# A persistent tile of weighted sums, two column groups visited per weight for two batches together, and another order of the head

## The chip, the cores and the metric

The kernel runs on one core of one Trainium2 chip. A core has a matrix engine (TensorE, PE in the profile, with its weight loads as PEld), a vector engine (DVE), a scalar engine (ACT), a general engine (POOL) and SyncE (SP), which only issues transfers. Each engine works through its own list of instructions in order and waits on semaphores for the others. The metric is the time of one execution on the device in microseconds (us), as a median of runs; the profile is of one execution of its own.

## The reference

A cross attention between a sequence and a small state, then a gated layer over all rows:

```python
def _attn_ref(x, state):                      # x (8, 8, 512, 64), state (8, 8, 32, 64)
    scores = scale * np.matmul(x, state.transpose(0, 1, 3, 2))
    scores = scores - scores.max(-1, keepdims=True)
    a = np.exp(scores)
    a /= a.sum(-1, keepdims=True) + 1e-09
    xread = np.matmul(a, state)
    ...                                       # the same the other way round: sread from x
    return np.concatenate([xread, sread], axis=2)

def _moe_ref(x, w_gate, w_val, w_out):        # x (4352, 512), d_ff 1536
    gate = 1.0 / (1.0 + np.exp(-(x @ w_gate)))
    val = x @ w_val
    return gate * val @ w_out
```

The rows of a batch are its 512 sequence positions and its 32 state positions, with the 8 heads side by side as 512 columns.

## The kernel before

**Reassociation.** The rows that go into the gated layer are softmax weights times state. The kernel doesn't form them for the sequence positions: for each batch it first multiplies the state with the gate and value weights (the tile `SW`, "weighted sums", 1536 columns for each of two sides `e` and each weight `w`), and then the softmax weights `aT` with `SW`. A block `f` of 128 hidden columns is then four matmuls of 128x512: two for the gate (`gvp`, first half) and two for the value.

**A visit** (`sw_visit`, through `sw_pair` or `sw_mm`) makes weighted sums of one batch: 8 matmuls, each on 64 rows and 32 columns of the array with 512 moving columns, into two PSUM banks; two copies (`sw_cp`, on ACT or DVE) bring them to `SW`. With `sw_pair` the 512 columns are 256 of the gate and the same 256 of the value weights, so a visit needs both weights. `sw_wide` makes three visits for 768 columns, for batch 2 in the head.

**A block** is `gv_mm` (or `gv_half` for one of its two halves), then `gv_th` (tanh on ACT), then `gv_glu` (DVE). The output product runs as seven products of sums and differences of quarter matrices: `h_sum` and `s_sum` build sums of the glu tile, `ht_sum` differences of the output weights, `h_mm` and `w_mm` the products, `w_add` and `w_keep` put them together.

**Softmax.** For batch 0 by quarters: `Sq_mm`, `Sq_exp`, `nq_sum`, `nq_mul`; for others by halves: `S_mm`, `S_exp`, `n_sum`, `n_mul`; `at_Eb` casts the exponentials on POOL (4 casts). `aT_mm` and `aT_cp` transpose the softmax weights on PE for batches 0 and 1; `aT_dma` does so by transfers on SP for later ones. `rd_mm` and `rd_fin` are the read of the state side.

**Loads.** All weights are loaded by POOL and cast on the way: `load_w(w, lo, n)` for n columns of the gate (0) or value (1) weights from column lo, `load_wo` for a third of the output weights, `load_sb` for two batches' states (transposed later by `sT_mm`). The columns come in the groups 256 (256 to 511), 1024, 0 and 1280 of 256 columns each, and 512 (512 to 1023).

**Order.** The schedule is manual: each engine runs its instructions in the order in which the list of calls in the kernel has them. The *head* is the long list from line 563 to line 837; it covers batches 0 and 1 and prepares batch 2. From there `step(b, f)` repeats for the batches 2 to 7 and the rows of all states. PSUM has eight banks, named G0, G1, OU, S0 to S3 and AT, and each call names its bank, so a call also waits for the one that last read its bank. In the profile L293 and L286 are visits, L343 the blocks of `gv_mm`, L355 those of `gv_half`, L442 the products of the head, L234 `aT_mm`, L543 `sT_mm`, L104 `load_w`, L527 `load_sb`, L107 `load_wo`, L200 `at_Eb`, L193 `nq_mul`, L227 `n_mul`, L111 the zeroing of a tile.

Of the kernel before, what the change touches and what calls it, by code (L numbers as in the profile page):

```python
# [8 lines left out]
FP = mybir.dt.float32  # L9
# [7 lines left out]
def kernel(  # L17
# [116 lines left out]
    def xT_cp(b, j, cp, n=1):  # L134
        cp(xT_tile(b)[:, j:j + n], held["xT", b, j])
# [161 lines left out]
    def sw_visit(b, lo, n, p0, p1, *ws):  # L297

        if b not in SWs:
            SWs[b] = fp.tile((128, 2, 2, dff), BF, name="SW", bufs=2)  # L300
        pss = [p[0].tile((128, 512), FP, name="swp", tag=p[1]) for p in (p0, p1)]
        if not ws:
            sw_pair(pss, b, lo, n)
            for e in range(2):
                sw_left[b, lo, 2, e] = (SWs[b][:, e, :, lo:lo + n], pss[e].rearrange("p (w n) -> p w n", w=2))
        for w in ws:
            sw_mm(pss, b, w, lo, n, 0)
            for e in range(2):
                sw_left[b, lo, w, e] = (SWs[b][:, e, w, lo:lo + n], pss[e][:, :n])

    def sw_wide(b, v, *places):

        if b not in SWs:
            SWs[b] = fp.tile((128, 2, 2, dff), BF, name="SW", bufs=2)
# [345 lines left out]
    gv_glu(0, 2)  # L660
    gv_mm(0, 9, AT, S3)
    gv_mm(1, 3, G1, S0)
    gv_th(0, 9)
    sw_cp(1, 1024, 2, 1, vec)
    gv_mm(1, 2, AT, G0)
    gv_glu(0, 9)
    gv_th(1, 3)
    gv_glu(1, 3)
    nc.scalar.activation(pre[:, 0:1], ones, AF.Exp)
    gv_th(1, 2)  # L670
    sT_mm(2, S1)
    gv_mm(1, 8, S2, S3)
    zero(sTz, pool)
    gv_th(1, 8)
    gv_glu(1, 2)
    load_x(2, nc.gpsimd)
    gv_mm(0, 8, S0, G0)
    sw_visit(0, 0, 256, AT, S2)
    sT_cp(2, vec)
    gv_glu(1, 8)  # L680
    sw_cp(0, 0, 2, 0, vec)
    gv_th(0, 8)
    sw_cp(0, 0, 2, 1, act)
    sw_visit(0, 1280, 256, S1, G1)
    sw_cp(0, 1280, 2, 1, act)
    sw_cp(0, 1280, 2, 0, vec)
    load_wo(0)
    gv_mm(1, 9, OU, S0)
    gv_th(1, 9)
    gv_glu(1, 9)  # L690
    gv_mm(0, 1, S2, S3)
    sT_mm(3, G1)
    sT_mm(1, AT)
    gv_th(0, 1)
    gv_glu(0, 1)
    sT_cp(3, act)
# [24 lines left out]
    gv_mm(0, 5, G1, OU)
    rd_fin(1)
    gv_th(0, 5)
    gv_mm(0, 7, S1, S3)
    sw_cp(1, 512, 1, 0, vec)
    sw_cp(1, 512, 1, 1, act)
    gv_glu(0, 5)
    nc.gpsimd.memset(xs[:, :, :, D:], 1.0)
    gv_mm(0, 4, S0, G0)
    gv_th(0, 7)  # L730
    gv_glu(0, 7)
    gv_th(0, 4)
    gv_glu(0, 4)
    gv_mm(0, 6, S1, G1)
    cast_x(2, pool, 4, 4)
    load_wo(2)
    gv_th(0, 6)
    sw_wide(2, 1, S3, OU, S0, G0, S2, AT)
    gv_glu(0, 6)
    sw_cp(2, 1, 0, 1, act)  # L740
    sw_cp(2, 1, 0, 0, vec)
    sw_cp(2, 1, 1, 1, vec)
    sw_cp(2, 1, 1, 0, act)
    gv_mm(1, 5, S1, G1)
    gv_th(1, 5)
    gv_glu(1, 5)
    sw_cp(2, 1, 2, 0, act)
    h_sum(0, 1, vec)
    gv_mm(1, 6, OU, S3)
    sw_visit(1, 1280, 256, S1, G0)  # L750
    gv_th(1, 6)
    sw_cp(2, 1, 2, 1, act)
    sw_visit(1, 0, 256, S2, S0)
    sw_cp(1, 1280, 2, 0, act)
    h_sum(2, 0, pool)
    h_sum(2, 1, vec)
    sw_cp(1, 1280, 2, 1, act)
    gv_mm(1, 4, G1, OU)
    gv_glu(1, 6)
# [17 lines left out]
    h_mm(5, 0, G1)
    S_mm(2, 0, OU)
    h_mm(5, 1)
    ht_sum(2, vec)  # L780
    h_sum(1, 0, vec)
    load_x(3, nc.sync)
    ht_sum(1, vec)
    gv_th(1, 10)
    h_mm(7, 0, S0)
    gv_glu(1, 10)
    sw_cp(1, 0, 2, 0, act)
    h_sum(3, 0, pool)
    w_keep('V1', 1)
    h_mm(6, 0)  # L790
    S_exp(2, 0)
    n_sum(2, 0)
    n_mul(2, 0, pool)
    S_mm(2, 1, G0)
    aT_dma(2, 0)
    S_exp(2, 1)
    gv_mm(1, 0, OU, S2)
    h_sum(3, 1, vec)
    gv_th(1, 0)
    h_mm(6, 1)  # L800
    w_keep('U2', 1)
    n_sum(2, 1)
    ht_sum(3, vec)
    n_mul(2, 1, pool)
    aT_dma(2, 1)
    h_U4()
    gv_mm(1, 1, G0, S1)
    h_mm(2, 0, S3)
    gv_glu(1, 0)
    h_mm(2, 1)  # L810
    gv_th(1, 1)
    cast_x(3, pool, 4, 4)
    h_mm(3, 0)
    gv_glu(1, 1)
    cast_x(3, pool, 0, 4)
    at_xT_dma(3)
    h_mm(7, 1)
    w_add(2, 'V1', w_res(0, 0)[:, :, lo_])
    h_mm(3, 1)
    sw_wide(2, 0, AT, S2, S1, G0, S3, OU)  # L820
    w_add(7, 'U4', w_res(0, 1)[:, :, hi_])
    sw_cp(2, 0, 1, 1, act)
    sw_cp(2, 0, 0, 1, act)
    sw_cp(2, 0, 2, 0, act)
# [10 lines left out]
    at_Eb(2)  # L835
    rd_mm(2, S2)
    rd_fin(2)

    order = {0: "1a", 1: "1b", 2: "2a", 3: "2b", 4: "6a", 5: "6b", 6: "5a", 7: "5b", 8: "7a7b", 9: "3a", 10: "3b4a", 11: "4b"}
    last_order = {0: "1a", 1: "1b", 2: "2a", 3: "2b", 4: "6a", 5: "6b", 6: "5a", 7: "5b", 8: "7a", 9: "7b", 10: "3a", 11: "3b"}  # L840

    def sw_six(b, v):

        if b not in SWs:
            SWs[b] = fp.tile((128, 2, 2, dff), BF, name="SW", bufs=2)
# [190 lines left out]
```

## Time and profile before

| | us |
|---|---|
| median of 3 runs (212.85 to 213.03) | 212.94 |
| the profiled execution | 213.18 |
| its span, first to last instruction | 211.4 |
| PE busy in the span (96%) | 203.4 |
| DVE busy (76%) | 160.5 |
| ACT busy (61%) | 129.8 |
| POOL busy (37%) | 78.6 |

The granted clock of TensorE is 1.00 throughout. A row of the timeline reads: start and duration in us, engine (a q behind it marks an engine's issue of a transfer that doesn't count as busy), line, operation, written tile <- read tiles, shape, number of instructions merged, and in brackets the idle time of the engine before it and what ended that. A row of the DMA issues has the size of one and the time from issue to landing. Matmuls overlap, so a row of many lasts longer than the distance to the next row.

### The profile page before, as it was taken

To read this page: it belongs to the slowest core of one execution; us is meant where nothing else is said; L and a number is where in the kernel's file an instruction comes from. 1 tells how busy PE (TensorE), PEld (TensorE's weight loads), DVE (VectorE), ACT (ScalarE), POOL (GpSimd) and SP (SyncE) were. 2 spreads that over 40 slices of the span, in tenths; PEclk is the share of its full clock that TensorE was granted. 3 is DMA by queue.
4 is the path that set the end of the run, shared out by engine and by line. 5 is a ranking of instruction groups with operands and counts; after the bars stand their busy time and mean duration, and the time that the engine had idled before them with its cause. 6 is when DMAs were issued, how large, how long until landed. Compare 5 with 4: busy or idle time off the path is not lost.

```text
span 211.4 us, 5331 instructions
## 1 busy us (share of the span) xinstructions
PE 203.4 (96%) x2089; PEld 132.1 (62%) x2089; DVE 160.5 (76%) x308; ACT 129.8 (61%) x244; POOL 78.6 (37%) x104
## 2 busy tenths in 40 slices
PE   7679999999999999999999999999999999999993
PEld 2445443677666656565656565656566666788982
DVE  2788889998987788578876887687848876864682
ACT  4978888754767477855786578647774673233210
POOL 8899358599042705900391029301500000000010
PEclk9999999999999999999999999999999999999999
DMA  6999999671689942995923611274110500130044
GB/s 205 180 192 191 227 277 179 113 214 38 80 220 349 123 93 85 301 104 141 312 65 48 195 78 28 58 110 164 29 31 0 202 2 0 74 128 0 3 172 125
DMA packets 40921, 27.14 MB, mean 128 GB/s; under 512 B 23617, under 2 KB 38721, under 8 KB 40897
## 3 DMA queue, kind: packets, MB, share of 16 engines
q1 hardware_dynamic: 30544, 19.47, 37.1%
q0 software_dynamic: 9920, 7.01, 20.4%
q10 hardware_dynamic: 432, 0.33, 0.6%
q8 instruction: 16, 0.26, 0.6%
q14 instruction: 9, 0.07, 0.2%
HBM read 18.35 MB, written 8.91 MB: 129 GB/s over the span
## 4 chain that ended last, share of the span: by engine, by line
PE 91%; DMA 4%; POOL 2%; issue 1%; DVE 0%; POOLq 0%
PE gvp L355 30%; PE outp L425 29%; PE gvp L343 10%; PE gvp L358 5%; PE outp L442 4%; DMA wgv<-in_moe_w_val_dram 4%; PE swp L286 4%; PE outp L484 2%; PE swp L293 2%; PE Sp L147 1%; PE outp L467 1%; POOL wgv L104 1%; PE rdp L262 1%; POOL xf L100 1%; PE rdp L265 0%
## 5 line engine op out<-in xcount | busy, mean ns | idle before, releaser
L369 DVE SCALAR_TENSOR_TENSOR glu<-th,gvp 128x512 bf16<-128x512 f32 (+1 forms) x108 | 70.1, 655 | 36.6 <-PE gvp L355 13.7
L364 ACT ACTIVATE th<-gvp 128x512 f32<-128x512 f32 (+1 forms) x108 | 62.1, 578 | 49.5 <-PE gvp L355 34.8
L355 PE MATMUL gvp<-aT,SW 128*128 128x512 bf16 x288 | 77.4, 379 | 0.1
L329 ACT CAST SW<-swp 128x512 bf16<-128x512 f32 x83 | 46.7, 593 | 9.3 <-PE swp L286 8.3
L425 PEld LDWEIGHTS <-Sm 128*128 128x128 bf16 x324 | 31.7, 98 | 12.6
L355 PEld LDWEIGHTS <-SW 128*128 128x128 bf16 x288 | 26.7, 98 | 17.3 <-issue 3.1
L200 POOL CAST Eb<-E 128x256 bf16<-128x256 f32 x32 | 12.8, 438 | 52.0 <-ACT E L167 52.0
L425 PE MATMUL outp<-tw,Sm 128*128 128x256 bf16 x240 | 31.8, 273 | 0.0
L425 PEld LDWEIGHTS <-glu 128*128 128x128 bf16 x240 | 23.5, 98 | 10.2
L425 PE MATMUL outp<-wo,glu 128*128 128x256 bf16 x168 | 22.9, 273 | 0.0
L343 PE MATMUL gvp<-aT,SW 128*128 128x512 bf16 x96 | 22.6, 379 | 0.0
L509 POOL DMA_DIRECT2D out_dram<-res x1 | 0.6, 613 | 50.3 <-DVE res L433 50.3
L227 POOL TENSOR_TENSOR ab<-E,ri 128x512 bf16<-128x512 f32 x13 | 14.3, 1100 | 11.8 <-DVE ri L210 7.1
L407 DVE TENSOR_TENSOR Sm<-glu 128x768 bf16<-128x768 bf16 (+1 forms) x34 | 18.0, 536 | 0.0
L433 DVE SCALAR_TENSOR_TENSOR res<-outp,U 128x512 f32<-128x512 f32 x22 | 15.1, 686 | 1.2 <-PE outp L442 0.9
L343 PEld LDWEIGHTS <-SW 128*128 128x128 bf16 x96 | 8.7, 98 | 10.5 <-issue 1.6
L116 POOL CAST xb<-xf 128x1024 bf16<-128x1024 f32 x12 | 13.2, 1126 | 2.3 <-DMA xf<-in_x_dram 2.3
L358 PE MATMUL gvp<-xb,wgv 128*128 128x256 bf16 x96 | 12.6, 273 | 0.0
L167 ACT ACTIVATE E<-Sp 128x512 f32<-128x512 f32 x14 | 8.4, 599 | 6.9 <-PE Sp L147 5.7
L425 PE MATMUL outp<-wo,Sm 128*128 128x256 bf16 x84 | 11.5, 273 | 0.0
L358 PEld LDWEIGHTS <-wgv 128*128 128x128 bf16 x96 | 9.3, 98 | 1.3
L251 POOL CAST xs<-xf 128x1024 bf16<-128x1024 f32 x10 | 10.1, 1039 | 0.0
(106 smaller groups left out, 221.6 us busy)
## 6 DMA issues: line engine op xcount, KB each, us to landing
out_dram<-res SPq DMA_DIRECT2D x14, 512.0 KB, 3.3
xf<-in_x_dram SPq DMA_DIRECT2D x5, 1024.0 KB, 7.5
wo<-in_moe_w_out_dram POOLq DMA_DIRECT2D x3, 512.0 KB, 8.1
xf<-in_x_dram SPq DMA_DIRECT2D x4, 256.0 KB, 3.7
wgv<-in_moe_w_gate_dram POOLq DMA_DIRECT2D x4, 256.0 KB, 7.3
wgv<-in_moe_w_val_dram POOLq DMA_DIRECT2D x4, 256.0 KB, 8.7
xf<-in_x_dram POOLq DMA_DIRECT2D x1, 1024.0 KB, 10.1
xf<-in_x_dram POOLq DMA_DIRECT2D x2, 256.0 KB, 5.9
```

The source lines that it names most:

```text
L116: cp(xbs[b].rearrange("p c h d -> p h c d")[:, lo:lo + n], (xhs if b in xhs else xfs)[b][:, lo:lo + n])
L200: nc.gpsimd.tensor_copy(Ebs[b][:, c], E1s[b][:, c])
L227: (nc.gpsimd if eng is pool else nc.vector).tensor_tensor(half(b, i, abs_), e1, ri.unsqueeze(len(ri.shape)).to_broadcast(e1.shape), ALU.mult)
L329: cp(*sw_left.pop((b, lo, w, e)))
L343: nc.tensor.matmul(ps, SWs[b][:, g, w, fs], aTs[b][:, :, g], start=(g == 0), stop=(g == 1))
L355: nc.tensor.matmul(ps, SWs[b][:, g, w, fs], aTs[b][:, :, g], start=(g == 0), stop=(g == 1))
L358: nc.tensor.matmul(ps, (wg, wv)[w][:, j, fs], held["XS"][:, j], start=(j == 0), stop=(j == 3))
L364: nc.scalar.activation(th, held["gv", b, f][0], AF.Tanh, scale=0.5)
L369: nc.vector.scalar_tensor_tensor(glus[b][:, f], held["th", b, f], 1.0, held["gv", b, f][1], ALU.add, ALU.mult)
L407: eng.tensor_tensor(S_(b, t)[:, i], a, c, op)
L425: nc.tensor.matmul(wps[key][:, c], lhs[:, i, c * 128:(c + 1) * 128], rhs[:, i], start=(first and c == 0 and i == 0), stop=(i == NF // 2 - ...
L433: nc.vector.scalar_tensor_tensor(to, wps[key], 0.5, held["w", name], ALU.mult, ALU.add)
```

## The change

- The tile `SWp`, which lives through the whole kernel, holds the weighted sums of two batches; batch b uses half b % 2. Before, `SW` was a tile of a pool with two buffers.
- `sw_joint(w, lo, ...)` visits 256 columns of one weight for the batches 0 and 1 together: 16 matmuls with 256 moving columns into two banks, and two copies into both halves of `SWp`. Four of these (gate and value, groups 256 and 1024) stand in place of four visits of the two batches.
- Blocks 3 and 2 of batch 0 are issued by halves (`gv_half`).
- The rest of the head has another order and other banks, and some operations change engines.

```diff
+    SWp = wp.tile((128, 2, 2, 2, dff), BF, name="SWp")
...
         if b not in SWs:
-            SWs[b] = fp.tile((128, 2, 2, dff), BF, name="SW", bufs=2)
+            SWs[b] = SWp[:, b % 2]
...
+    def sw_joint(w, lo, p0, p1):
+
+        pss = [p[0].tile((128, 2, 256), FP, name="swp", tag=p[1]) for p in (p0, p1)]
+        for b in range(2):
+            SWs[b] = SWp[:, b]
+            for j in range(4):
+                for e in range(2):
+                    rows = slice(e * 64, (e + 1) * 64)
+                    nc.tensor.matmul(pss[e][j * Ns:(j + 1) * Ns, b], sTd[rows, b, 2 * j + e, e],
+                                     (wg, wv)[w][rows, j, lo:lo + 256], start=True, stop=True)
+        for e in range(2):
+            sw_left["j", lo, w, e] = (SWp[:, :, e, w, lo:lo + 256], pss[e])
```

The head as it is after the change, up to the read of batch 1 (lines with a plus are new at their place; the lines that they replace are left out here), and of what follows the lines that change engines or banks:

```diff
     Sq_mm(0, 2, S1)
+    Sq_mm(0, 0, G1)
+    warm(3, S0)
+    xT_cp(0, 1, vec)
+    Sq_mm(0, 1, S3)
+    xT_mm(0, 3, AT)
+    load_w(0, 256, 256)
+    Sq_exp(0, 0)
+    xT_mm(1, 0, OU, 2)
+    Sq_exp(0, 1)
+    xT_cp(0, 3, vec)
     Sq_exp(0, 2)
     load_w(1, 256, 256)
+    Sq_mm(0, 3, S3)
+    xT_cp(1, 0, vec, 2)
     load_w(0, 1024, 256)
+    load_w(1, 1024, 256)
+    S_mm(1, 0, S0)
     nq_sum(0, 2)
+    Sq_exp(0, 3)
+    nq_sum(0, 3)
+    S_exp(1, 0)
+    xT_mm(1, 2, G0, 2)
+    at_Eb(0)
+    rd_mm(0, G1)
+    nq_mul(0, 2, pool)
+    sw_joint(0, 256, OU, S2)
     nq_sum(0, 0)
     nq_sum(0, 1)
+    nq_mul(0, 3, vec)
+    n_sum(1, 0)
+    nq_mul(0, 0, pool)
+    xT_cp(1, 2, act, 2)
+    nq_mul(0, 1, pool)
+    sw_cp("j", 256, 0, 1, act)
+    S_mm(1, 1, S0)
+    sw_joint(1, 256, S3, G0)
+    load_sb(2)
+    aT_mm(0, AT)
+    rd_fin(0)
+    S_exp(1, 1)
+    sw_cp("j", 256, 0, 0, act)
+    aT_cp(0, 1, act)
+    sw_cp("j", 256, 1, 1, act)
+    sw_cp("j", 256, 1, 0, act)
+    aT_cp(0, 0, vec)
     load_w(1, 0, 256)
+    sw_joint(0, 1024, S0, G1)
+    gv_half(0, 3, 0, AT)
+    n_sum(1, 1)
+    gv_th(0, 3)
+    n_mul(1, 1, vec)
+    sw_cp("j", 1024, 0, 0, act)
     load_w(1, 1280, 256)
+    gv_half(0, 2, 0, S2)
+    sw_joint(1, 1024, G0, S1)
+    n_mul(1, 0, pool)
+    sw_cp("j", 1024, 1, 0, act)
+    gv_half(0, 3, 1, S3)
+    sw_cp("j", 1024, 0, 1, vec)
+    sT_mm(2, AT)
     load_w(0, 1280, 256)
+    aT_mm(1, OU)
+    gv_th(0, 2)
     load_w(0, 0, 256)
+    sw_cp("j", 1024, 1, 1, vec)
+    sT_cp(2, vec)
+    gv_mm(0, 8, G1, G0)
+    aT_cp(1, None, vec)
+    nc.scalar.activation(pre[:, 0:1], ones, AF.Exp)
     load_sb(1)
+    gv_mm(0, 9, S1, S2)
+    gv_glu(0, 3)
+    gv_th(0, 8)
+    gv_th(0, 9)
+    gv_mm(1, 3, S0, S3)
+    gv_half(0, 2, 1, G1)
+    gv_mm(1, 8, OU, AT)
+    gv_glu(0, 8)
+    at_Eb(1)
+    gv_glu(0, 9)
     load_sb(3)
+    gv_th(1, 3)
+    gv_glu(0, 2)
+    gv_th(1, 8)
+    gv_mm(1, 2, S1, G0)
     load_w(0, 512, 512)
+    sw_visit(0, 1280, 256, S2, S0)
+    gv_th(1, 2)
+    gv_glu(1, 3)
+    zero(sTz, pool)
+    sw_visit(0, 0, 256, OU, S3)
+    gv_mm(1, 9, G1, S1)
+    sw_cp(0, 0, 2, 0, act)
+    gv_glu(1, 8)
+    sT_mm(3, AT)
+    sw_cp(0, 0, 2, 1, vec)
     load_w(1, 512, 512)
+    sT_mm(1, OU)
+    gv_th(1, 9)
     sw_cp(0, 1280, 2, 1, act)
     sw_cp(0, 1280, 2, 0, vec)
+    sT_cp(1, act)
+    gv_mm(0, 0, S3, S2)
+    gv_mm(0, 1, G1, S0)
+    load_x(2, nc.gpsimd)
+    gv_glu(1, 2)
+    gv_th(0, 0)
+    sw_visit(0, 512, 512, S3, OU, 0)
+    gv_glu(1, 9)
+    sT_cp(3, vec)
+    gv_th(0, 1)
+    sw_visit(1, 512, 512, G0, S1, 0)
+    gv_mm(0, 10, G1, AT)
+    sw_cp(0, 512, 0, 0, act)
+    gv_glu(0, 0)
+    sw_cp(0, 512, 0, 1, vec)
+    gv_mm(0, 11, S3, S2)
     load_wo(0)
+    sw_cp(1, 512, 0, 1, act)
+    sw_cp(1, 512, 0, 0, act)
     gv_glu(0, 1)
+    sw_visit(0, 512, 512, S1, OU, 1)
+    gv_th(0, 11)
     gv_th(0, 10)
+    sw_visit(1, 512, 512, S0, G0, 1)
+    sw_cp(0, 512, 1, 1, vec)
+    sw_cp(0, 512, 1, 0, act)
+    nc.gpsimd.memset(xs[:, :, :, D:], 1.0)
+    rd_mm(1, S3)
+    rd_fin(1)
...
+    h_sum(2, 1, pool)
...
+    ht_sum(2, pool)
...
+    n_mul(2, 0, pool)
...
+    h_sum(3, 1, pool)
...
+    h_mm(7, 0, S0)
...
+    gv_glu(1, 1)
+    sw_wide(2, 0, OU, S3, G0, S2, S1, AT)
...
+    n_mul(2, 1, vec)
...
-    h_sum(2, 1, vec)
...
-    ht_sum(2, vec)
...
-    h_sum(3, 1, vec)
...
-    n_mul(2, 1, pool)
...
-    sw_wide(2, 0, AT, S2, S1, G0, S3, OU)
...
```

More of the change, by code (lines that the diff above doesn't have):

```diff
@@ L313, in sw_wide @@
         if b not in SWs:
-            SWs[b] = fp.tile((128, 2, 2, dff), BF, name="SW", bufs=2)
+            SWs[b] = SWp[:, b % 2]
         lo = 768 * v
@@ L670 @@
[L670 to L684, printed above, removed]
+    sw_visit(0, 1280, 256, S2, S0)
[5 more added lines that the diff above has]
+    sw_cp(0, 0, 2, 0, act)
@@ L731 @@
+    load_wo(1)
+    gv_mm(0, 7, G1, OU)
+    gv_th(0, 7)
+    pad(2, 6)
+    gv_glu(0, 11)
+    gv_mm(0, 4, G0, S1)
     gv_glu(0, 7)
     gv_th(0, 4)
-    gv_glu(0, 4)
[L734 to L738, printed above, removed]
-    gv_glu(0, 6)
-    sw_cp(2, 1, 0, 1, act)
[L741 to L747, printed above, removed]
+    load_wo(2)
@@ new lines @@
+    gv_mm(0, 5, S3, S0)
+    cast_x(2, pool, 0, 4)
+    gv_mm(0, 6, S2, AT)
+    gv_th(0, 5)
+    gv_th(0, 6)
+    cast_x(2, pool, 4, 4)
+    gv_glu(0, 4)
+    gv_glu(0, 5)
+    at_xT_dma(2)
+    sw_wide(2, 1, S1, OU, G1, G0, S0, S2)
+    gv_glu(0, 6)
+    gv_mm(1, 5, S3, AT)
+    sw_cp(2, 1, 0, 0, vec)
+    sw_cp(2, 1, 1, 1, act)
+    gv_mm(1, 7, G0, S1)
+    gv_th(1, 5)
+    gv_th(1, 7)
+    sw_cp(2, 1, 2, 0, vec)
+    sw_cp(2, 1, 2, 1, vec)
+    gv_mm(1, 4, S3, G0)
+    sw_cp(2, 1, 1, 0, act)
@@ L748 @@
+    gv_glu(1, 5)
+    gv_glu(1, 7)
+    sw_visit(1, 1280, 256, S2, G1)
+    gv_th(1, 4)
+    sw_visit(1, 0, 256, AT, S0)
+    gv_mm(1, 6, S3, S1)
+    sw_cp(1, 1280, 2, 1, vec)
+    sw_cp(2, 1, 0, 1, act)
+    gv_glu(1, 4)
+    S_mm(2, 0, OU)
+    h_sum(2, 1, pool)
+    sw_cp(1, 1280, 2, 0, act)
     h_sum(0, 1, vec)
-    gv_mm(1, 6, OU, S3)
-    sw_visit(1, 1280, 256, S1, G0)
+    load_x(3, nc.sync)
+    gv_mm(1, 11, G1, G0)
     gv_th(1, 6)
-    sw_cp(2, 1, 2, 1, act)
-    sw_visit(1, 0, 256, S2, S0)
@@ L777 @@
[L777 to L799 removed]
+    h_sum(0, 0, pool)
+    h_mm(2, 0, S2)
@@ new lines @@
+    ht_sum(0, vec)
+    gv_th(1, 11)
+    h_sum(1, 0, pool)
+    h_mm(1, 0, S3)
+    h_mm(1, 1)
+    sw_cp(1, 0, 2, 1, act)
+    S_exp(2, 0)
+    h_sum(1, 1, vec)
+    w_keep('V1', 1)
+    h_sum(3, 0, pool)
+    S_mm(2, 1, OU)
+    ht_sum(2, pool)
+    h_mm(2, 1)
+    h_mm(5, 0, G1)
+    ht_sum(1, vec)
+    n_sum(2, 0)
+    gv_glu(1, 11)
+    w_add(2, 'V1', w_res(0, 0)[:, :, lo_])
+    h_sum(2, 0, vec)
+    sw_cp(1, 0, 2, 0, act)
+    h_mm(5, 1)
+    n_mul(2, 0, pool)
+    S_exp(2, 1)
+    h_sum(3, 1, pool)
@@ L800 @@
+    n_sum(2, 1)
+    h_mm(6, 0)
+    gv_glu(1, 6)
     h_mm(6, 1)
     w_keep('U2', 1)
-    n_sum(2, 1)
+    cast_x(3, pool, 0, 4)
+    gv_mm(1, 0, S2, OU)
+    h_U4()
+    gv_th(1, 0)
+    gv_mm(1, 10, S0, G0)
+    gv_th(1, 10)
+    gv_mm(1, 1, S1, AT)
+    h_mm(7, 0, S0)
+    aT_dma(2, 0)
+    gv_th(1, 1)
+    gv_glu(1, 0)
+    gv_glu(1, 10)
+    gv_glu(1, 1)
+    sw_wide(2, 0, OU, S3, G0, S2, S1, AT)
+    h_mm(7, 1)
+    h_mm(3, 0)
+    n_mul(2, 1, vec)
     ht_sum(3, vec)
-    n_mul(2, 1, pool)
@@ L844, in sw_six @@
         if b not in SWs:
-            SWs[b] = fp.tile((128, 2, 2, dff), BF, name="SW", bufs=2)
+            SWs[b] = SWp[:, b % 2]
         lo = 768 * v
```

143 lines of the change are left out of this document (5 added, 138 removed).

## The prediction

> **What bounds the kernel now.** I read the page first, then stretches of the span, then TensorE (PE) in order of time, then POOL and the DMA issues. The profiled execution took 213.18 us around this span, 0.24 us over the median of 212.94:
>
> ```profile
> span 211.4 us, 5331 instructions
> ```
>
> Busy time by stretch (PE, PEld, DVE, ACT, POOL, then granted clock, DMA share, GB/s):
>
> ```profile
> 16.00:28.00 12.00, 12.00 (x115) 5.46 (x100) 10.18 (x17) 9.92 (x21) 8.36 (x12) 1.00 1.37 231
> 28.00:54.00 26.00, 25.98 (x343) 15.59 (x343) 23.97 (x43) 17.93 (x35) 19.26 (x20) 1.00 0.73 149
> ...
> 34.00:35.00 1.00, 1.00 (x6) 0.41 (x6) 1.00 (x3) 1.00 (x3) 1.00 (x2) 1.00 0.73 87
> 35.00:36.00 1.00, 1.00 (x20) 0.33 (x18) 1.00 (x3) 1.00 (x3) 0.96 (x1) 1.00 1.19 184
> 36.00:37.00 1.00, 1.00 (x20) 0.36 (x5) 1.00 (x3) 1.00 (x4) 0.52 (x1) 1.00 1.25 206
> ```
>
> From 16 us to the end of the head (54 us) PE has no idle time: any stall that the new order adds there is paid in full, and there is nothing to win there by waiting less. What can be won lies before 16 us. PE in order of time, and the one weight load (PEld) that waited for a transfer:
>
> ```profile
> 15.62 0.63 PE L293 MATMUL swp<-wgv,tw 64*32 64x512 bf16 x16 [0.27 <-DMA wgv<-in_moe_w_val_dram]
> 16.18 0.62 PE L234 MATMUL aTp<-ident,ab 128*128 128x128 bf16 x8
> 16.64 3.62 PE L343 MATMUL gvp<-aT,SW 128*128 128x512 bf16 x16
> 20.09 0.40 PE L543 MATMUL stp<-ident,tw 128*128 128x64 bf16 x8
> 20.32 1.89 PE L343 MATMUL gvp<-aT,SW 128*128 128x512 bf16 x8
> 22.14 0.62 PE L293 MATMUL swp<-wgv,tw 64*32 64x512 bf16 x16
> ...
> 28.03 1.05 PE L286 MATMUL swp<-wgv,tw 64*32 64x512 bf16 x24
> ```
>
> ```profile
> 28.46 0.14 PEld L286 LDWEIGHTS <-tw 64*32 64x32 bf16 x16 [0.31 <-DMA wgv<-in_moe_w_val_dram]
> ```
>
> So the dense stretch starts at 15.62, when the value columns 1024 land, and at 28.46 PE meets a transfer again: value columns 512 to 1023, the largest load. At that point the kernel is just in time. Everything after 28.46 is the same work in both kernels.
>
> **What POOL issues, and when.** POOL issues all weight loads, in the order of the list:
>
> ```profile
> 7.28 0.74 POOL L527 DMA_DIRECT2D tw<-in_state_dram  x1
> 8.01 0.77 POOL L104 DMA_DIRECT2D wgv<-in_moe_w_val_dram  x1
> 9.35 1.19 POOL L193 TENSOR_TENSOR ab<-E,riq 128x256 bf16<-128x256 f32 x2 [0.57 <-DVE riq L188]
> 10.48 0.81 POOL L104 DMA_DIRECT2D wgv<-in_moe_w_val_dram  x1
> 11.28 1.42 POOL L200 CAST Eb<-E 128x256 bf16<-128x256 f32 x4
> 12.65 0.74 POOL L104 DMA_DIRECT2D wgv<-in_moe_w_gate_dram  x1
> 13.41 1.06 POOL L227 TENSOR_TENSOR ab<-E,ri 128x512 bf16<-128x512 f32 x1
> 14.40 0.80 POOL L104 DMA_DIRECT2D wgv<-in_moe_w_gate_dram  x1
> 15.21 1.47 POOL L527 DMA_DIRECT2D tw<-in_state_dram  x2
> 16.67 0.77 POOL L104 DMA_DIRECT2D wgv<-in_moe_w_gate_dram  x1
> 17.40 0.79 POOL L104 DMA_DIRECT2D wgv<-in_moe_w_val_dram  x1
> 18.13 1.47 POOL L200 CAST Eb<-E 128x256 bf16<-128x256 f32 x4
> 19.50 1.84 POOL L111 MEMSET sTz<- 128x2048 bf16 x1
> ```
>
> **The change, part by part.**
>
> *Joint visits.* Four visits of 8 matmuls of 512 columns become four of 16 matmuls of 256: the columns that stream stay the same (two old visits, x16, take 0.56 us: 15.62 to 16.18). Eight copies of 128x512 stay eight copies of 128x512. What changes is that a visit needs one weight alone. The four first weight loads keep their places on POOL, so the value columns 1024 still land at about 15.5 and release the last joint visit at about 15.62. By then the new order has done the gate visit of 1024 as well (0.2 to 0.3 us gained) and four matmuls of the hidden layer (the gate halves of blocks 3 and 2), as many as before (both halves of block 3).
>
> *PE from 15.62.* Joint visit with its change of tile shape 0.56, one half block 0.43 (16 matmuls from 16.64 to 20.09 give 0.216 each, so 0.43 for a half and 0.86 for a block), the state transpose 0.23, the transposes of the softmax weights 0.46, five and a half blocks 4.75: 22.05, against 22.14 before with the same seven blocks done. The head start is eaten by the change of shape for one more visit. Taken as nothing; bounds -0.3 and +0.3 (ACT, which makes most of the copies here, would be late by half a copy). From there: two visits 0.56, a block 0.86, two state transposes 0.47, two blocks 1.73, so the gate visits of the columns 512 are wanted at 25.8; with their 0.56 and two blocks 1.73, the value visits at 28.2. Before, they ran at 28.46. Mode changes are as many as before; the warm matmuls stay three.
>
> *POOL, the step that decides.* Behind the fourth weight load the list now has the four casts of Eb, three multiplications instead of two, and only then the load of the second state group. The casts wait for the last quarter exponential. Before, two of these ended at 9.53:
>
> ```profile
> 8.66 0.87 ACT L182 ACTIVATE E<-Sp 128x256 f32<-128x256 f32 x2
> ```
>
> The new order has the same four at about the same place, so 9.6. Then: casts 1.42, multiplications 3 x 0.595 = 1.79: 12.8. State load 0.74, two value loads 0.77 + 0.81: 15.1. The batch 1 multiplication 1.06: 16.2. Two gate loads 0.74 + 0.80, a state load 0.74: 18.5. Casts of batch 1 1.47: 19.95. State load 0.74, gate 512 load 0.77: issued at 20.7, over at 21.5. The zeroing of sTz 1.84: the value 512 load is issued at 23.3 instead of 17.40. Behind it stand the input of batch 2 and the three output weight loads, which come later by 2 to 3 us at most and are queued in the DMA stream anyway.
>
> How long does such a load take when the stream isn't full? Issue to landing of the loads of 512 KB (gate 512, value 512, the last of the output weights):
>
> ```profile
> wgv<-in_moe_w_gate_dram POOLq DMA_DIRECT2D x1, 512.0 KB, 8.1
> ```
>
> ```profile
> wgv<-in_moe_w_val_dram POOLq DMA_DIRECT2D x1, 512.0 KB, 11.0
> ```
>
> ```profile
> wo<-in_moe_w_out_dram POOLq DMA_DIRECT2D x1, 512.0 KB, 6.4
> ```
>
> ```profile
> 32.34 0.74 POOL L107 DMA_DIRECT2D wo<-in_moe_w_out_dram  x1
> ```
>
> The first two were queued behind others. The third is the nearest: issued at 32.34, with the stream running dry before it (87 GB/s in 34 to 35, 206 in 36 to 37), it took 6.4 us. So value 512 lands between 23.3 + 6.4 = 29.7 and, if I take off 1.2 us for tails and an earlier POOL, 28.5; gate 512 at 26 to 27.1 instead of wanted 25.8, a stall which the second wait swallows. I take 29.4, so the value visits start at 29.45: +1.0 us against 28.46. Bounds 0 (backlog hides the late issue) and +1.6.
>
> The Trainium skill, "DMA: Bandwidth & Descriptors", section "Anatomy of one DMA — SWDGE (gpsimd) path", gives about 2.0 us and the bytes at 436 GB/s for one such load. For 1 MB read, that is an estimate of 4.4 us by that page, hence 27.7 and no wait at all; the 6.4 us measured here speak against it, and I go by the row.
>
> *The head behind 28.46.* The same blocks, products and visits, at the same PE cost. What moves: one sum of the glu tiles (768 columns) and one difference of the output weights (1536 columns) from DVE to POOL, one multiplication from POOL to DVE.
>
> ```profile
> 42.35 2.29 POOL L407 TENSOR_TENSOR Sm<-glu,Sm 128x768 bf16<-128x768 bf16 x1 [2.39 <-DVE Sm L407]
> ```
>
> ```profile
> 39.98 1.82 DVE L400 TENSOR_TENSOR tw<-wo 128x1536 bf16<-128x1536 bf16 x2
> ```
>
> ```profile
> L369 DVE SCALAR_TENSOR_TENSOR glu<-th,gvp 128x512 bf16<-128x512 f32 (+1 forms) x108 | 70.1, 655 | 36.6 <-PE gvp L355 13.7
> ```
>
> On DVE the difference cost 0.91; on POOL, at twice the 2.29 of half its width, up to 4.6, with about 2 us to spare before product 7 needs it. DVE is at 23.97 of 26 us in this stretch, and the second wide visit now ends on bank AT, which waits for the last glu operation (0.66) of batch 1: 0.2 us, bounds 0 and 0.6. The second transposes of batch 2's softmax weights go out on SP behind a multiplication that now sits late on DVE; before, the block that needs them started here:
>
> ```profile
> 53.57 0.61 PE L355 MATMUL gvp<-aT,SW 128*128 128x512 bf16 x2
> ```
>
> That start moves with PE; taken as nothing, bounded by 0 and 0.3.
>
> *The persistent tile SWp* replaces two rotating buffers of the same size: nothing, since each batch still has its half.
>
> **Sum.** 213.18 + 1.0 + 0.2 = 214.4 for the profiled execution; 0.24 less for the median: 214.1 us.
>
> **The rivals.**
> - *The late issue is hidden* (0.18). If backlog keeps the stream full until the value 512 load is in it, it lands by 28.4. For this: the load took 11.0 us of which most was queueing, and at 206 GB/s its bytes need only 2.5 us. Against: POOL's own sum puts its issue 5.9 us later. Time: 212.9 plus 0 to 0.2. The rule of the Trainium skill quoted above ("DMA: Bandwidth & Descriptors") would lead here.
> - *Faster* (0.12). The joint visits by gate alone give PE the 0.3 us before 15.6, and the value 512 load lands before 28.0, since POOL gets through its list by 22 us (casts and multiplications in cover of waits). Then the old wait is gone as well and the head start stays: 212.94 - 0.45 = 212.5. It decides at a landing of 28.0; against it stands the sum of POOL's rows.
> - *Slower by much more* (0.15). The lateness passes on: the output weights land later too, the differences on DVE and POOL start later, and the products wait for them. Another 1 us behind the 1.2: 215.1.
> - The forecast itself has 0.55.
>
> A difference under 0.2% (0.43 us) is about what a measurement of this kernel can't tell from no change. Slower by more: 0.55 + 0.15 = 0.70; within: 0.18; faster: 0.12. The range goes from 212.7, which takes in the hidden case, to 215.3, which takes in most of the worst; the forecast's own range is 213.5 to 214.8.
>
> **What would show it.** In the changed profile: POOL issues the value 512 load at about 23 us; the stream has a dip between 15 and 24 us; PE has a wait for gate 512 or value 512 between 25.8 and 29.8, of about 1 us together; the last joint visit starts at about 15.6 and seven blocks are done by 22.1. I'm wrong if the value 512 load is issued before 21 us, if it lands by 28.4 in spite of its late issue, if PE loses over 0.4 us before 22 us on ACT's copies, or if more than 0.6 us go between 30 and 54 us.

## The result, and the profile after

| | before | after |
|---|---|---|
| median, us | 212.99 (212.85 to 213.55) | 220.23 (219.56 to 220.9) |
| the profiled execution, us | 213.18 | 220.9 |
| its span, us | 211.4 | 219.0 |

The ratio after to before is 1.0326, 95% interval 1.0291 to 1.0361: 7.2 us slower, where 1.1 were predicted. The direction was right, the size far outside the range. The profiled execution is the slowest of the four.

The page of the kernel after, its span, PE's busy time and the granted clock in 40 slices:

```profile
span 219.0 us, 5382 instructions
...
PE 206.8 (94%) x2121; PEld 133.2 (61%) x2121; DVE 164.9 (75%) x309; ACT 128.7 (59%) x241; POOL 84.0 (38%) x106
...
PEclk9999889999999999999999999999999999999999
```

Two of the slices show an 8, a granted clock of 0.8 to 0.9, which no slice did before. The stretches, as before (PE, PEld, DVE, ACT, POOL, then granted clock, DMA share, GB/s):

```profile
16.00:28.00 12.00, 10.18 (x95) 5.04 (x95) 9.65 (x16) 6.92 (x14) 10.66 (x16) 0.90 1.33 173
...
25.60:29.00 3.40, 3.40 (x23) 1.77 (x22) 2.57 (x5) 2.27 (x5) 1.71 (x4) 0.50 1.23 226
...
28.00:54.00 26.00, 22.99 (x236) 11.77 (x234) 22.80 (x33) 16.33 (x32) 17.66 (x12) 0.98 0.88 172
```

PE, which had no idle time from 16 to 54 us, stood idle for 1.8 us before 28 and for 3.0 us behind it. The transfers moved 173 GB/s in 16 to 28 us against 231: the dip that late loads leave. For 3.4 us the clock was at half. That is a matter of this execution: 3.4 us at half clock in 219 take 0.008 off an execution's mean granted clock, which is 0.992 here and 1.0, 0.999 and 1.0 in the other three, and these took 220.84, 219.62 and 219.56 us all the same. PE in order of time up to the value visits of the columns 512:

```profile
15.13 1.02 PE L369 MATMUL gvp<-aT,SWp 128*128 128x512 bf16 x4 [0.78 <-ACT SWp L343]
16.09 0.41 PE L337 MATMUL swp<-wgv,tw 64*32 64x256 bf16 x16
...
22.70 0.41 PE L294 MATMUL swp<-wgv,tw 64*32 64x512 bf16 x8
24.85 0.41 PE L294 MATMUL swp<-wgv,tw 64*32 64x512 bf16 x8 [1.74 <-DMA wgv<-in_moe_w_gate_dram]
...
30.00 0.63 PE L287 MATMUL swp<-wgv,tw 64*32 64x512 bf16 x16
...
32.39 0.62 PE L287 MATMUL swp<-wgv,tw 64*32 64x512 bf16 x16
```

The first visits after the dense blocks come at 22.70 (22.14 before). The second of them, of the columns 0, waits for its gate weights (gate 0 below). The gate visits (30.00) and value visits (32.39) of the columns 512, for which the prediction reckoned 1.0 of its loss of 1.2 us, wait for nothing any more: PE arrives too late for that. In this execution the value visits are 3.93 us behind those of before (28.46): 0.56 at the joint visits, 1.93 at the columns 0 (two visits in 2.49 instead of 0.56), an estimated 1.7 for 3.4 us at half clock, and the remainder, 0.26 less, for the other order.

PE from there to the read of batch 2:

```profile
32.95 0.42 PE L266 MATMUL rdp<-xf,Eb 128*32 128x64 bf16 x32
...
42.54 0.29 PE L148 MATMUL Sp<-sTz,xT 128*128 128x64 bf16 x4 [0.42 <-DMA xT<-xb]
43.03 0.29 PE L148 MATMUL Sp<-sTz,xT 128*128 128x64 bf16 x4 [0.20 <-DMA xT<-xb]
...
50.20 1.47 PE L456 MATMUL outp<-tw,Sm 128*128 128x256 bf16 x12 [1.85 <-DVE tw L414]
52.20 2.94 PE L357 MATMUL gvp<-aT,SWp 128*128 128x512 bf16 x12 [0.53 <-DVE res L447]
...
60.22 0.42 PE L266 MATMUL rdp<-xb,Eb 128*32 128x64 bf16 x32
```

From the read of batch 1 to that of batch 2 the work is the same in number, 23.11 us before (29.02 to 52.13) and 27.27 after: 4.16 us more. The waits for the transposes of batch 2's input (0.62), for the differences of the output weights on DVE (1.85) and for a result on DVE (0.53) make up 3.0 of it; the rest lies in longer matmul rows and small gaps for which the trace names no cause. Behind 60.22 the kernel after is 0.49 us shorter. 3.93 + 4.16 - 0.49 is 7.6, the difference of the spans.

The loads on POOL went as forecast within 0.5 us, the value 512 load at 23.40 (forecast 23.3):

```profile
16.55 1.56 POOL L105 DMA_DIRECT2D wgv<-in_moe_w_gate_dram  x2
...
20.92 0.77 POOL L105 DMA_DIRECT2D wgv<-in_moe_w_gate_dram  x1
21.65 1.85 POOL L112 MEMSET sTz<- 128x2048 bf16 x1
23.40 0.79 POOL L105 DMA_DIRECT2D wgv<-in_moe_w_val_dram  x1
```

What made the later part slow stands in DVE and POOL side by side:

```profile
41.46 1.64 POOL L421 TENSOR_TENSOR Sm<-Sm,glu 128x768 bf16<-128x768 bf16 x1
41.64 0.68 DVE L383 SCALAR_TENSOR_TENSOR glu<-th,gvp 128x512 bf16<-128x512 f32 x1
42.23 1.28 DVE L421 TENSOR_TENSOR Sm<-glu 128x768 bf16<-128x768 bf16 x1
43.18 1.83 POOL L421 TENSOR_TENSOR Sm<-glu,Sm 128x768 bf16<-128x768 bf16 x1
43.44 2.39 DVE L414 TENSOR_TENSOR tw<-wo 128x1536 bf16<-128x1536 bf16 x1
44.98 3.80 POOL L414 TENSOR_TENSOR tw<-wo 128x1536 bf16<-128x1536 bf16 x1
45.75 3.44 DVE L421 TENSOR_TENSOR Sm<-Sm,glu 128x768 bf16<-128x768 bf16 x1
49.11 0.94 DVE L414 TENSOR_TENSOR tw<-wo,tw 128x1536 bf16<-128x1536 bf16 x1
```

A sum of 128x768 that took DVE 3.44 us beside POOL's difference takes 0.55 alone; a difference of 128x1536 took 2.39 instead of 0.94. Each stretched DVE operation ends a little after POOL's: 43.51 after 43.10, 45.83 after 45.01, 49.19 after 48.78. The glu at 41.64, which reads PSUM, was not stretched (0.68). In these pairs POOL's operation was the first to start. The kernel before has a pair the other way round, and the prediction shows one half of it, POOL's sum of 2.29 at 42.35:

```profile
42.18 0.95 DVE L400 TENSOR_TENSOR tw<-wo,tw 128x1536 bf16<-128x1536 bf16 x1
```

There DVE started first and took its usual time, and POOL's sum, 1.64 at 33.34 and 38.32 of the same list, took 2.29. So the mutual hold-up could be read in the kernel before.

### The profile page after: what moved, and what is told of

It reads as the page before. It is cut to its first block, busy times and chain, and to the rows that moved or that the text cites. A ratio compares the mean times of both kernels' runs of the same rounds, so it can differ in the third digit from the quotient of the medians.

```text
span 219.0 us, 5382 instructions
## 1 busy us (share of the span) xinstructions
PE 206.8 (94%) x2121; PEld 133.2 (61%) x2121; DVE 164.9 (75%) x309; ACT 128.7 (59%) x241; POOL 84.0 (38%) x106
## 4 chain that ended last, share of the span: by engine, by line
PE 77%; DMA 9%; DVE 6%; POOL 4%; ACT 1%; issue 1%; DVEq 0%; POOLq 0%
PE gvp L369 29%; PE outp L439 28%; DMA wo<-in_moe_w_out_dram 6%; PE gvp L372 5%; DMA wgv<-in_moe_w_gate_dram 3%; PE swp L287 3%; PE outp L498 2%; DVE Sm L421 2%; PE warm L531 2%; PE outp L456 2%; PE swp L294 1%; DVE tw L414 1%; PE gvp L357 1%; PE outp L481 1%; PE Sp L148 1%; POOL wgv L105 1%
## 5 line engine op out<-in xcount | busy, mean ns | idle before, releaser
L369 PE MATMUL gvp<-aT,SWp 128*128 128x512 bf16 x296 | 79.7, 379 | 0.8 <-ACT SWp L343 0.8
L343 ACT CAST SWp<-swp 128x512 bf16<-128x512 f32 x83 | 46.7, 591 | 11.5 <-PE swp L287 8.2
L369 PEld LDWEIGHTS <-SWp 128*128 128x128 bf16 x296 | 27.4, 98 | 18.9 <-issue 4.0
L201 POOL CAST Eb<-E 128x256 bf16<-128x256 f32 x32 | 14.0, 471 | 55.2 <-ACT E L168 52.6
L357 PE MATMUL gvp<-aT,SWp 128*128 128x512 bf16 x88 | 22.1, 396 | 0.6 <-DVE res L447 0.5
L421 DVE TENSOR_TENSOR Sm<-glu 128x768 bf16<-128x768 bf16 (+1 forms) x34 | 18.8, 554 | 0.0
L228 POOL TENSOR_TENSOR ab<-E,ri 128x512 bf16<-128x512 f32 x12 | 12.6, 1052 | 13.4 <-DVE ri L211 8.7
L357 PEld LDWEIGHTS <-SWp 128*128 128x128 bf16 x88 | 8.3, 101 | 11.3 <-issue 3.6
L421 DVE TENSOR_TENSOR Sm<-Sm,glu 128x768 bf16<-128x768 bf16 (+1 forms) x17 | 11.9, 699 | 0.3
L343 DVE CAST SWp<-swp 128x512 bf16<-128x512 f32 x13 | 8.6, 684 | 3.8 <-PE swp L294 2.2
## 6 DMA issues: line engine op xcount, KB each, us to landing
wo<-in_moe_w_out_dram POOLq DMA_DIRECT2D x3, 512.0 KB, 12.1
```

Of the source, the lines that this page charges most:

```text
L201: nc.gpsimd.tensor_copy(Ebs[b][:, c], E1s[b][:, c])
L228: (nc.gpsimd if eng is pool else nc.vector).tensor_tensor(half(b, i, abs_), e1, ri.unsqueeze(len(ri.shape)).to_broadcast(e1.shape), ALU.mult)
L357: nc.tensor.matmul(ps, SWs[b][:, g, w, fs], aTs[b][:, :, g], start=(g == 0), stop=(g == 1))
L369: nc.tensor.matmul(ps, SWs[b][:, g, w, fs], aTs[b][:, :, g], start=(g == 0), stop=(g == 1))
L421: eng.tensor_tensor(S_(b, t)[:, i], a, c, op)
```

## The experiments

Theory: two losses that the prediction missed. (1) The late loads stop PE at the columns 0 already, and the stop costs a stretch at half clock on top (e3 and e4 speak against this second half). (2) POOL's sums and differences hold DVE's up, DVE is late, and products wait. Rivals: the joint visits themselves; a loss from the late loads alone that is carried on to the end.

**e1, loads early.** In the kernel after, three loads go ahead of the casts of batch 0.

```diff
+    load_sb(2)
+    load_w(1, 0, 256)
+    load_w(1, 1280, 256)
     at_Eb(0)
...
-    load_sb(2)
...
-    load_w(1, 0, 256)
...
-    load_w(1, 1280, 256)
```

> The changed kernel with three loads (state group 2, value columns 0 and 1280) issued in POOL's idle 2.6 us ahead of the casts of Eb. Theory 'late loads': the stream no longer runs dry, the 1.9 us wait at the visit of columns 0, the 3.4 us at half clock (1.7 us lost) and the wait for batch 2's transposes (0.9 us) go; the waits behind 46 us (2.0, 0.7 and 0.4 us, put down to POOL and DVE working at once) stay: 220.2 - 4.5 = 215.7 us, 215 to 216.5. Rival 'lateness is the whole cause': the later waits go too, 212.5 to 213.5. Rival 'the new order itself' (joint visits, banks): stays above 218.

Measured 216.92 us (216.74 to 217.1), ratio to before 1.0177 (1.0162 to 1.0192), 3.3 below the kernel after and above the expected range. The first and last reads and the remaining waits:

```profile
28.76 0.42 PE L266 MATMUL rdp<-xf,Eb 128*32 128x64 bf16 x32
39.11 0.29 PE L148 MATMUL Sp<-sTz,xT 128*128 128x64 bf16 x4 [1.18 <-DMA xT<-xb]
...
46.01 1.47 PE L456 MATMUL outp<-tw,Sm 128*128 128x256 bf16 x12 [1.09 <-DVE tw L414]
...
56.04 0.42 PE L266 MATMUL rdp<-xb,Eb 128*32 128x64 bf16 x32
```

The first part is back to before's (28.76 against 29.02), with the clock full, and the later part takes 27.28 us, as in the kernel after (27.27). The wait for the transposes, which the expectation took to go, is longer and the one for DVE shorter (1.18 and 1.09 against 0.42 and 1.85): the difference that PE waits for last ends on DVE 17.10 us behind the read of batch 1 in both. The two losses are separate; the lateness isn't passed on.

**e2, the same with the difference of the output weights on DVE.** `ht_sum(2)` goes back to DVE, and `n_mul(2, 1)` to POOL.

```diff
-    ht_sum(2, pool)
+    ht_sum(2, vec)
...
-    n_mul(2, 1, vec)
+    n_mul(2, 1, pool)
```

> As the one before, and the difference of output weights number 2 goes back from POOL to DVE, the last softmax multiplication of batch 2 back from DVE to POOL. Theory 'late loads and the difference on POOL': both gone, 213.0 us, 212.5 to 213.6. Rival 'the new order itself' has a share: over 214.5. Rival 'lateness is the whole cause': the same as the kernel before this one within 0.4 us.

Measured 215.54 (215.38 to 217.38), ratio 1.014 (1.0092 to 1.0188): better than e1 by 1.4, though their intervals overlap, and 2.5 above the expectation. POOL and DVE there, then PE:

```profile
39.31 1.83 POOL L421 TENSOR_TENSOR Sm<-glu,Sm 128x768 bf16<-128x768 bf16 x1
39.57 2.39 DVE L414 TENSOR_TENSOR tw<-wo 128x1536 bf16<-128x1536 bf16 x1
```

```profile
39.44 0.29 PE L148 MATMUL Sp<-sTz,xT 128*128 128x64 bf16 x4 [1.19 <-DMA xT<-xb]
```

POOL's other sums still hold DVE up, and the transposes, issued from 33.10, leave PE waiting until 39.44.

**e3, the same edit with the loads left late.**

> The changed kernel with the loads as they are; only the difference of output weights number 2 back on DVE and the last multiplication of batch 2 back on POOL. Theory 'late loads and the difference on POOL': 220.2 - 2.5 = 217.7 us, 217 to 218.5, and the DVE sum of 768 columns that took 3.44 us takes about 0.6. Rival 'lateness is the whole cause': 220 within 0.5 us.

Measured 218.25 (217.34 to 220.34), ratio 1.0254 (1.0191 to 1.0316), 2.0 us below the kernel after, as expected; again the intervals overlap, and no more than the direction follows. Its lists are those of the kernel after until behind the transposes, so its trace shows a second execution of that part:

```profile
24.17 0.41 PE L294 MATMUL swp<-wgv,tw 64*32 64x512 bf16 x8 [0.79 <-DMA wgv<-in_moe_w_gate_dram]
...
42.02 0.29 PE L148 MATMUL Sp<-sTz,xT 128*128 128x64 bf16 x4 [2.15 <-DMA xT<-xb]
```

Here the stop at gate 0 was 0.79 and the clock stayed full behind it. PE read batch 1 at 30.70 instead of 32.95, met the transposes nearly where the kernel after does (42.02 against 42.54), waited 2.15 for them and ran at about half clock after that. So of the 2.25 us that it was earlier, 0.52 were left at the transposes: they land late, and take up what PE gains ahead of them.

**e4, the wait kept warm.** Seven dummy matmuls stand where PE waits for gate 0.

```diff
+    warm(7, OU)
     sw_visit(0, 0, 256, OU, S3)
```

> The changed kernel with seven warm matmuls (1.5 us) put before the visit of columns 0, where PE waits 1.7 us. Theory: the granted clock stays 1.00 through 25 to 29 us and 1.5 us come back: 218.7 us, 218.3 to 219.2. Rival: the half clock costs nothing since PE would wait for the next loads anyway: 220.2 within 0.4 us; or the clock falls in spite of them: 220.2 to 220.5.

Measured 219.71 (218.97 to 221.44), ratio 1.032 (1.0272 to 1.0368): no difference from the kernel after that can be told. Two stretches and two rows of PE:

```profile
24.00:28.00 4.00, 3.94 (x40) 1.92 (x38) 2.54 (x5) 2.44 (x5) 2.82 (x5) 1.00 1.24 203
43.10:46.50 3.40, 3.40 (x17) 1.80 (x14) 3.40 (x2) 1.58 (x3) 3.40 (x2) 0.51 1.02 312
```

```profile
30.84 0.63 PE L287 MATMUL swp<-wgv,tw 64*32 64x512 bf16 x16
...
42.35 0.29 PE L148 MATMUL Sp<-sTz,xT 128*128 128x64 bf16 x4 [1.78 <-DMA xT<-xb]
```

The clock was full at 24 to 28 and the value visits came 1.55 us earlier (30.84). That the dummies did it isn't shown, since e3 had full clock there without them. PE then met the transposes at the old place (42.35 against 42.54), waited longer, and the half clock came there instead. The gain was given back.

**e5, only the loads late.** The kernel before, with POOL's order as in the change: group 2's state and the values 0 and 1280 behind the casts of batch 0, the casts of batch 1 ahead of the last state and the gate 512 load, and the zeroing ahead of the value 512 load.

> The kernel before, with nothing of the change but POOL's order of loads: the loads of state group 2 and of value columns 0 and 1280 behind the casts of Eb, the casts of batch 1 ahead of state group 3, the zeroing of sTz ahead of value 512. Theory 'late loads': PE waits about 2 us at the visits of columns 0 and 1280 and some more at those of 512, the clock may halve for 3.4 us (1.7 us), and batch 2's input and the output weights land 2 to 3 us later: 213 + 3.5 = 216.5 us, 215 to 218. Rival 'the new order itself' (late loads matter only together with it): 213 to 213.8.

Measured 214.64 (213.95 to 215.97), ratio 1.0072 (1.005 to 1.0095). In before's order the late loads cost 1.5 us (214.64 against 213.11 of the kernel before, measured beside it), below the 2 us that this expectation had as its least and within the prediction's bound. The profiled execution, the slowest of the eight, has the wait that the prediction named:

```profile
31.26 0.62 PE L286 MATMUL swp<-wgv,tw 64*32 64x512 bf16 x16 [0.86 <-DMA wgv<-in_moe_w_val_dram]
```

Its visits of the columns 0 and 1280 run with no wait of their own, and the clock stays at 1.0. But PE reaches them at 23.88 only, 1.74 us later than before, with waits of 1.1 us for DVE at the transposes of the input and of 0.6 for ACT. Whether an execution without that delay would stop at gate 0 this trace can't say.

**e6, only the difference on POOL.** One word in the kernel before.

```diff
-    ht_sum(2, vec)
+    ht_sum(2, pool)
```

> The kernel before, with the difference of output weights number 2 on POOL instead of DVE and nothing else. Theory 'POOL and DVE slow each other in these operations': the DVE sum of 768 columns beside it takes about 3.4 us instead of 0.55, and with the other waits 213 + 1.5 = 214.5 us, 214 to 216. Rival 'POOL's operation is only long': DVE durations stay at 0.55 and 0.95, 213.0 to 213.6.

Measured 217.46 (216.83 to 218.81), ratio 1.019 (1.0163 to 1.0217): 4.35 us (217.46 against 213.11) for one operation, nearly three times the expectation. POOL and DVE, then PE, then the stretch behind it:

```profile
41.63 3.09 POOL L400 TENSOR_TENSOR tw<-wo 128x1536 bf16<-128x1536 bf16 x1
41.69 3.84 DVE L400 TENSOR_TENSOR tw<-wo 128x1536 bf16<-128x1536 bf16 x1
```

```profile
45.58 1.38 PE L442 MATMUL outp<-tw,Sm 128*128 128x256 bf16 x6 [2.60 <-DVE tw L400]
```

```profile
45.70:49.10 3.40, 3.40 (x23) 2.53 (x22) 2.72 (x6) 0.60 (x1) 2.28 (x1) 0.50 0.63 219
```

The difference that DVE kept went from 0.95 to 3.84 us and ended 0.81 after POOL's. PE waited 2.60 us for it and then ran 3.4 us at half clock, worth an estimated 1.7: 4.3 us together. The profiled execution took 218.81, as its input came late and another stretch of half clock followed that, at 12 to 15 us; from the read of batch 1 to that of batch 2 it took 27.53 us (30.73 to 58.26) against 23.11 before, 4.42 more, near the 4.35 of the medians. The other three executions have a mean granted clock of 0.991 or 0.992, about one such stretch each.

**e7, the scores later.** e2, with `S_mm(2, 0)` moved from ahead of all products to behind the first two halves, and `S_mm(2, 1)` behind one half more.

> The kernel e2_loads_early_sum_dve with the scores of batch 2 behind two and four products of the head instead of ahead of them. Theory: their wait for the transposing transfers (1.35 and 0.38 us in its profile) goes since PE has products to do meanwhile: 215.5 - 1.6 = 213.9 us, 213.5 to 214.4. Rival: the transposes only land when the loads of the output weights end, and so do those that the products need, so the wait moves to the products: 215 to 215.6.

Measured 215.69 (215.15 to 215.94), ratio 1.0114 (1.0091 to 1.0136): no gain. The wait for the transposes is gone and two others are as long:

```profile
44.60 1.47 PE L456 MATMUL outp<-tw,Sm 128*128 128x256 bf16 x12 [0.80 <-DVE tw L414]
46.60 2.92 PE L357 MATMUL gvp<-aT,SWp 128*128 128x512 bf16 x12 [0.53 <-DVE res L447]
```

The time is the rival's (up to 215.6), the mechanism isn't quite: PE waits for DVE, whose list runs without a gap from 38.06 to 44.46, and not for the loads. DVE was the next limit behind the transposes. **e8** added to e7 a single copy of batch 0's transposed weights on DVE, product 7 ahead of the wide visit, and an earlier multiplication.

> The same, and three small moves: the transposed softmax weights of batch 0 copied by DVE alone (PE waited 1.06 us for a DVE copy that waited for ACT's copy from the same bank), product 7's second half ahead of the wide visit (0.34 us wait for bank AT), batch 2's last multiplication ahead of POOL's casts of batch 3. Theory: 213.9 - 0.5 - 0.3 = 213.1 us, 212.6 to 213.6, about level with the kernel before. Rival: the head start meets the loads of gate 0 and value 512 and is lost in waits there: 213.6 to 214.

Measured 215.56 (214.86 to 217.58), ratio 1.0126 (1.0071 to 1.0182): these three bring nothing that can be told, where 213.1 was expected.

**e9, the joint visits alone.** The kernel before with the four joint visits at the places of its four visits, and with the tile alone.

> The kernel before with only the persistent tile and the four joint visits put at the places of its four visits; list, engines, loads and casts otherwise as before. If the loss sits in the order of loads, the idle stretch and the DVE/POOL overlap, this costs nothing and may give the 0.2 to 0.3 us by which the gate visit no longer waits for the value columns: 212.7 to 213.2 us, ratio 0.999 to 1.001. Rival: the joint visits themselves cost (their copies go to both batches, so block 3 of batch 0 waits for more copies on ACT): 213.5 to 214.2.

> The kernel before with only the persistent tile in place of the two rotating buffers. Both theories: nothing, 213.0 plus or minus 0.2. A loss of 0.5 us or more would say that the tile itself orders work that the rotating buffers left free.

The tile alone: 213.17 (212.83 to 215.22), ratio 1.0018 (0.9999 to 1.0037), nothing. The joint visits: 214.78 (214.53 to 215.22), ratio 1.0083 (1.0071 to 1.0096), against my theory. PE shows where:

```profile
19.98 2.12 PE L357 MATMUL gvp<-aT,SWp 128*128 128x512 bf16 x9 [1.23 <-DVE SWp L343]
```

A joint copy holds both batches, so block 9 of batch 0 needs all four copies of the columns 1024; the last, which before was batch 1's alone and not urgent, stands far down DVE's list. **e11** moves that one copy up:

```diff
+    sw_cp("j", 1024, 1, 1, vec)
     aT_cp(1, None, vec)
...
-    sw_cp("j", 1024, 1, 1, vec)
```

> The kernel e9_before_joint with the last of the four copies of the columns 1024 moved ahead on DVE, before the copy of batch 1's softmax weights. In e9_before_joint block 9 of batch 0 waits 1.23 us for this copy, since a joint copy holds the sums of both batches. If that wait is the whole price of the joint visits, it goes: 213.1 to 213.7 us. Rival: the joint visits cost by themselves (more changes of the array's tile shape, copies on ACT later): 214.3 or more.

Measured 213.37 (213.0 to 215.11), ratio 1.0005 (0.9979 to 1.0031), and the same blocks run through:

```profile
17.03 3.62 PE L357 MATMUL gvp<-aT,SWp 128*128 128x512 bf16 x16
```

So the joint visits cost and win nothing that can be told; a copy in the wrong place costs 1.4 us (214.78 to 213.37; 1.7 by the ratios), 1.23 of it the wait.

**e10, sums apart.** e7 with the two sums that POOL made beside DVE's put on DVE.

```diff
-    h_sum(1, 0, pool)
+    h_sum(1, 0, vec)
...
-    h_sum(3, 0, pool)
...
     ht_sum(1, vec)
+    h_sum(3, 0, vec)
```

> The kernel e7 with the two sums of the glu tile that POOL still makes while DVE makes sums and differences (first halves of sums 1 and 3) put on DVE, 0.55 us each. Theory that DVE and POOL slow each other: DVE gains 0.73 and 1.48 us on its two stretched operations and pays 1.1, so product 6 (1.0 us late behind the difference of the output weights) and the wait behind it (0.7) go: 214.0 to 214.6 us. Rival, that DVE is simply full in this stretch and any sum put on it comes back as a wait: 215.7 or more.

Measured 214.63 (214.11 to 217.39), ratio 1.0074 (1.0054 to 1.0093): 1.06 us less than e7 by the medians, 0.9 by the ratios, whose intervals just overlap, for more work on DVE. Its profiled execution took 217.39 and met late loads, so only DVE's durations are read from it:

```profile
39.80 0.55 DVE L421 TENSOR_TENSOR Sm<-glu 128x768 bf16<-128x768 bf16 x1
42.08 0.96 DVE L414 TENSOR_TENSOR tw<-wo 128x1536 bf16<-128x1536 bf16 x1 [1.73 <-issue]
```

The same two took 1.28 and 2.39 in e7. No kernel tried beats the one before.

## Why the prediction was wrong

- *POOL, the step that decides.* The issue times were right to 0.5 us, that of value 512 to 0.1, and the cause was right: e5 gives 1.5 us for it in before's order, within the bound of 1.6. One thing failed. The 6.4 us of a 512 KB load were used for the columns 512 only, while the smaller loads in front of them were taken to be in time. In the kernel after these were no faster than that:

```profile
wgv<-in_moe_w_gate_dram POOLq DMA_DIRECT2D x4, 256.0 KB, 7.2
...
wgv<-in_moe_w_val_dram POOLq DMA_DIRECT2D x1, 512.0 KB, 7.4
```

  Gate 0 was issued as the second of the two at 16.55, so at about 17.3, and took 7.5. The prediction's own figures have it issued at 16.9 and wanted at 22.3 (22.05 and half of two visits); with 6.4 us it lands at 23.3, a stop of 1.0 that was there to be read. The 4.4 us estimated from the Trainium skill, "DMA: Bandwidth & Descriptors", section "Anatomy of one DMA — SWDGE (gpsimd) path", are far from the 7.4 measured for value 512, which had other loads in front of it. A small slip besides: the prediction's terms give 25.7 and 28.0 for the visits of the columns 512, not 25.8 and 28.2; its sum doesn't use them.
- *The clock* was taken as 1.00 throughout because it was so before. In the profiled execution a stop of 1.74 us was followed by 3.4 us at half clock. What this adds to the median isn't shown: three of the four executions had no such stretch, and in e3 and e4 the time that PE had won ahead of the transposes went into the wait for them. In e6 all four executions show the loss of clock, and there it is part of the price.
- *Term "the head behind 28.46", +0.2 with bounds 0 and 0.6*, is the step most wrong: 4.16 us. The price of POOL's own difference was within its bound ("up to 4.6", measured 3.80 and 3.09; the 2.29 that it was doubled from was itself held up by DVE), and the fallacy was to weigh it against PE's need alone ("2 us to spare before product 7"). What it did to DVE, which makes the other differences, was not priced; e6 prices it at 4.35 us by itself, e10 at about another 1 for two sums. The second loss in this part, the wait for the transposes, has two roots. The prediction let the output weights land later as "queued in the DMA stream anyway", and the transposes on SP end behind them: the last of these loads landed at 38.7 before (32.34 and 6.4) and at 42.1 after (29.99 and 12.1), the first of these transposes took 3.5 us before and 6.1 after. Their rows on SP, before and after:

```profile
35.99 5.21 SPq L140 DMA_TRANSPOSE xT<-xb  x4
```

```profile
36.36 5.54 SPq L141 DMA_TRANSPOSE xT<-xb  x4
```

  And PE asks for them sooner: the first scores of batch 2 stood behind three halves of products, and the change has them ahead of all, 9.2 us of work behind the read of batch 1 instead of 12.7. Against e2, e7 takes the wait away by the order alone.
- *PE from 15.62, taken as nothing with bounds of 0.3*: 0.56 late at 22.70, with the wait of 0.78 for ACT's copies at 15.13, which the text named as a sign of error. e9 and e11 show the size of such a misplaced copy (1.4) and no cost of the visits themselves that can be told; e9's tile alone bears out *SWp* at nothing.
- *Rivals.* "Slower by much more" named the lateness that passes on. It went another way: e1's later part is as slow as that of the kernel after with the loads in time. "Hidden" and "faster" needed value 512 by 28.4; it was issued at 23.40 and took 7.4.

The shares don't add up as medians, since a wait that goes lets the next one show (e4, e7): loads early 3.3, the difference back on DVE 1.4 and the sums apart about 1 leave 1.6 us above before. Built up from the kernel before, late loads alone cost 1.5 and the one difference 4.35, of 7.2. What the rest is was not tried; e7's trace still has the wait for a result on DVE (0.53) in it, and its first part is 0.35 us late (read of batch 1 at 29.37 against 29.02 before).

## What to carry to other kernels

Before an operation on SBUF tiles goes from DVE to POOL, look at what DVE runs in the same microseconds: if these are sums of two SBUF tiles, add POOL's time, for as long as the two overlap, to the one that starts later, and follow that to PE. When loads are issued later, set every load's landing against its own consumer, the small ones too, then look for the next thing that PE meets behind a stop, since a later wait can hide what the stop cost. A stop near 2 us may bring 3.4 us of half clock with it; the mean granted clock of the other executions tells whether that is the rule or one execution. Where one copy now feeds two consumers, put it where the earlier of the two needs it.

## What the runs showed of the hardware

- DVE's sums of two SBUF operands make next to no progress while a sum that POOL started earlier runs: they ended 0.41, 0.82, 0.41 and 0.81 us after POOL's, less than the 0.55 and 0.95 that they need alone. Where DVE started first, it took its 0.95, and POOL 2.29 instead of 1.64. The Trainium skill, "GPSIMD Engine Reference", section "Key points", says that the two share their SBUF interfaces and contend where DVE has two SBUF inputs; the trace agrees and adds the size.
- The half clock came in stretches of 3.4 us, after stops of 1.74 and 2.60 us, and e4's after 1.78. The wait of 1.85 at 50.20 of the kernel after, and those of 1.19 in e2 and 1.23 in e9, were followed by none, so the length of the stop alone doesn't decide; nor does the program, since of the kernel after one execution in four had a stretch. The Trainium skill, "TensorE: Matmul & The Clock Gate", Part 1, describes a free-running window of about 3.4 us; the length of the stretches agrees, and a window that doesn't start with the stop would explain why equal stops differ, which no run here tests.
- The first transposes on SP landed 0.4 to 0.8 us behind the last load of the output weights in each trace read for it: 39.5 behind 38.7 before, 42.5 behind 42.1 after, 39.4 behind 39.0 in e2, where they were issued 2.9 us earlier than before (33.10 against 35.99) and took 6.3 us instead of 3.5. That the loads hold them up is argued from this; no run takes the loads away.
